# One transpose in place of two for the probabilities of a head, in the attention of a three-layer kernel

## The chip, the cores and the metric

One core of a Trainium2 chip runs the whole kernel. The metric is device microseconds of one execution; the time of a kernel is the median of its executions. The engines are TensorE (PE, with its weight loads shown apart as PEld), VectorE (DVE), ScalarE (ACT), GpSimd (POOL) and SyncE (SP), which issues most transfers.

## The reference

Three layers follow one another: attention with a sink and a sliding window, a mixture of eight experts with one expert a token, and a dense two-layer network.

```python
batch, n_heads, seq, head_dim = (2, 8, 768, 64); n_sink, window = (4, 128)
scores = scale * np.matmul(q, k.transpose(0, 1, 3, 2))
is_sink = pos[None, :] < n_sink
rel = pos[:, None] - pos[None, :]
in_window = (rel >= 0) & (rel < window)
scores = np.where(is_sink | in_window, scores, -1000000000.0)
a = softmax(scores)                        # over the keys
x = np.matmul(a, v)                        # to [1536 tokens, 512]
...
expert_idx = np.argmax(xn @ en.T / tau, axis=1)
out[mask] = gate_w * (np.maximum(x[mask] @ w1[e], 0) @ w2[e])   # for each expert e
...
h = x @ w_in
y = np.maximum(0.01 * h, h) @ w_out
```

## The kernel before

Attention works on units. A unit is one batch b, one group g of four heads and one block i of 128 queries: 2 x 2 x 6 = 24 units, of four heads each, 96 items. With a window of 128, a query block sees two key blocks, its own and the one before; block 0 sees its own alone; blocks 2 to 5 see the sink keys too, which take 32 columns more. `SPAN[i]` says where the keys of block i begin, how many there are, which mask belongs to them, at which columns the key blocks stand (`cols`) and where the sink's columns are.

For an item, `score` makes two TensorE matmuls into `sc` (L276), VectorE adds the mask and takes the extreme into `p` and `los` (L281), and ScalarE takes the exponential in place (L285). `p` holds the four heads of a unit (four buffers). For blocks 2 to 5 GpSimd copies the sink's columns of the four heads together into `sp` (L290), which `flip_sink` turns (L307). `flip` turns each key block of a head with a TensorE transpose into `t` in PSUM (L299), two heads to a tile, and copies the tile to `pt` (L302), by ScalarE for the first pair of heads and by VectorE for the second. `value` multiplies `pt` by the values, eight matmuls of 65 columns and one for the sink (L317, L320). VectorE divides (L329 to L331), and the result is a row block of x, which goes to memory and through the router (`xTp` L729, `lg` L749).

The head's queries and keys are turned beforehand (`tk`, `tq` L206) and split into two parts by ScalarE and VectorE (`head_k` L212 and L217, `head_q` L226 and L229); GpSimd copies `raw_q` (L172) and the sink keys (L220). `stir` issues filler matmuls of 512 columns on a zero tile `warm` in the first steps (L362). `slot_u` (L780) are comparison tables of the router on GpSimd.

The loop over the 96 items is written with lags: at step s, item s is scored, item s - 5 is flipped (`LAG1`), the sink of item s - 7 is turned, and the unit whose last head is item s - 10 is multiplied by the values (`LAG2`). `later(n, fn)` puts a piece of work n steps on. In attention a scheduler then sets the order of each engine's queue from this program; from the experts on TensorE's order is that of the program. The order of units is batch 0 group 0, group 1, then batch 1 in halves; within a group blocks 1 to 5, then 0.

After attention come routing, eight experts (`hp` and `acc`, L1230, L1330, L1348), whose weights SyncE loads into slots as TensorE frees them (L1138, L1181, L1448), and the dense network, which ends the kernel.

`pick` decides, by limits on the inputs, whether a general path runs at the end; with these inputs it does not.

Of the kernel before, what the change touches and what calls it, by code (L numbers as in the profile page):

```python
# [7 lines left out]
F32 = mybir.dt.float32  # L8
F32R = mybir.dt.float32r
BF16 = mybir.dt.bfloat16  # L10
# [5 lines left out]
ALU = mybir.AluOpType  # L16
# [5 lines left out]
P = 128  # L22
# [6 lines left out]
SINK = 32  # L29
# [31 lines left out]
LAG1, LAGS, LAG2, PTB, PB = 5, 7, 10, 6, 4  # L61
HALFK = 3 * P
BEHIND = HALFK + SINK
# [85 lines left out]
def attention(c, ctx):  # L149
# [3 lines left out]
    nc, tc = c.nc, c.tc  # L153
    att = ctx.enter_context(tc.tile_pool(name="a_qk", bufs=4))
    wk = ctx.enter_context(tc.tile_pool(name="a_wk", bufs=2))
    psc = ctx.enter_context(tc.tile_pool(name="ps_sc", bufs=3, space=PSUM))
    c.psc = psc
    pst = c.pst = ctx.enter_context(tc.tile_pool(name="ps_t", bufs=4, space=PSUM))
# [80 lines left out]
    def group_turns(b, g):  # L239
# [4 lines left out]
    load_qk(0, 0, 0, 3)  # L244
    load_qk(0, 1, 0, 3)
    copied = c.copied
    c.warm = c.setting.tile([P, 512], BF16, name="warm")
    nc.vector.memset(c.warm, 0.0)
    setup(c)
    W3 = 2 * P + SINK  # L250


    SPAN = [(0, P, c.m0, [0], None), (0, 2 * P, c.m1, [0, P], None), (P, W3, c.ma, [0, P], 2 * P),
            (2 * P, W3, c.mb, [0, P + SINK], P), (HALFK, W3, c.mc, [SINK, P + SINK], 0),
            (BEHIND + P, W3, c.ma, [0, P], 2 * P)]
    units = {}
    after = []

    def later(n, fn):

        if n == 0:
            return fn()
        after.append((step[0] + n, c.uid(), fn))

    def score(b, g, i, h):
        if h == 0:
            u = units[b, g, i] = Ctx()
            u.p = wk.tile([P, 4, W3], F32, tag="p", name=f"p{b}{g}{i}", bufs=PB)
            u.pt = {}
        u = units[b, g, i]  # L270
        off, n, m, _, s0 = SPAN[i]
        kt, qt = heads[b, 4 * g + h]
        sc = psc.tile([P, W3], F32, tag="sc", name=f"sc{b}{g}{i}{h}")
        w = max(n, 2 * P)
        for half in range(2):
            nc.tensor.matmul(sc[:, 0:w], lhsT=qt[:, half, i * P:(i + 1) * P], rhs=kt[:, off:off + w],  # L276
                             start=half == 0, stop=half == 1)
        p = u.p[:, h, 0:n]
        col = ((b * 2 + g) * QB + i) * 4 + h
        lo = c.los[:, col:col + 1]  # L280
        c.scored = nc.vector.tensor_tensor_reduce(out=p, in0=sc[:, 0:n], in1=m, scale=1.0, scalar=3.0e38,  # L281
                                                  op0=ALU.add, op1=ALU.min, accum_out=lo)

        def raised():
            c.raised = nc.scalar.activation(out=p, in_=p, func=AF.Exp, scale=-1.0, bias=lo)  # L285

        later(1, raised)
        if h == 3 and i >= 2:
            u.sp = wk.tile([P, 4, SINK], F32, tag="sp", name=f"sp{b}{g}{i}")
            later(2, lambda: nc.gpsimd.tensor_copy(u.sp, u.p[:, :, s0:s0 + SINK]))  # L290

    def flip(b, g, i, h):
        u = units[b, g, i]
        cols = SPAN[i][3]
        nb = len(cols)
        if h % 2 == 0:
            u.t = pst.tile([P, 2, nb, P], F32, tag="t", name=f"tp{b}{g}{i}{h}")
        for n, o in enumerate(cols):
            nc.tensor.transpose(u.t[:, h % 2, n, :], u.p[:, h, o:o + P], c.ident)  # L299
        if h % 2 == 1:  # L300
            pt = u.pt[h // 2] = wk.tile([P, 2, nb, P], F32, tag="pt", name=f"pt{b}{g}{i}{h}", bufs=PTB)
            (nc.scalar.copy if h == 1 else nc.vector.tensor_copy)(out=pt, in_=u.t)  # L302

    def flip_sink(b, g, i):
        u = units[b, g, i]
        sk = pst.tile([P, P], F32, tag="t", name=f"sk{b}{g}{i}")
        nc.tensor.transpose(sk, u.sp.rearrange("p h s -> p (h s)"), c.ident)  # L307
        u.ps = wk.tile([P, P], F32, tag="ps", name=f"ps{b}{g}{i}")
        nc.scalar.copy(out=u.ps, in_=sk)
# [47 lines left out]
    def stir(n):  # L357
        if not n:
            return
        t = psx.tile([P, 512], F32, tag="x", name=f"stir{c.uid()}")  # L360
        for _ in range(n):
            nc.tensor.matmul(t, lhsT=c.warm[:, 0:P], rhs=c.warm, start=True, stop=True)  # L362

    items = [(b, g, i, h) for b, g, j0, j1 in UNITS for i in TURN[b][j0:j1] for h in range(4)]
    step = [-1]
# [6 lines left out]
    router_tables(c)  # L372
    setting = router_setup(c)
    stir(7)
    n = len(items)
    for m in (2, 0, 2):
        turn[0, 0][0].pop(0)()
        stir(m)
    s = 0
    while s < n or after:  # L380
# [5 lines left out]
        if s < n:  # L386
            b, g, i, h = items[s]
            if s in STIR:
                stir(STIR[s])
            for (nb, ng), at in FETCH.items():  # L390
                for half in range(2):
                    if s == at[half]:
                        load_qk(nb, 2 * ng, 3 * half, 3)
                        load_qk(nb, 2 * ng + 1, 3 * half, 3)
                if s == at[0]:
                    turn[nb, ng] = group_turns(nb, ng)
                if s == at[2]:
                    load_v(nb, ng)
            for k, at in TURNS.items():
                for half in range(2):  # L400
                    if s in at[half]:
                        turn[k][half].pop(0)()
            score(b, g, i, h)
            if s == 1:
                with tc.issue_after(copied.ins):
                    c.others()
        if 0 <= s - LAG1 < n:
            flip(*items[s - LAG1])
# [11 lines left out]
def pick(c, T, over):  # L420

    nc = c.nc
    part, big, ok = T([P, 1], "part"), T([P, 1], "big"), T([P, 4], "ok")
    nc.vector.tensor_reduce(out=part, in_=c.los, axis=AX.X, op=ALU.max)
    rows = c.ptr.tile([P, P], F32, tag="tr", name="rows_ps")
    nc.tensor.matmul(rows, lhsT=part.to_broadcast([P, P]), rhs=c.ident, start=True, stop=True)
    nc.vector.tensor_reduce(out=big, in_=rows, axis=AX.X, op=ALU.max)
    ns, win = c.ints[:, 0:1], c.ints[:, 1:2]  # L430
    nc.vector.tensor_scalar(out=ok[:, 0:1], in0=ns, scalar1=float(SINK), scalar2=None, op0=ALU.is_le)
    nc.vector.tensor_scalar(out=ok[:, 1:2], in0=win, scalar1=float(P + 1), scalar2=ok[:, 0:1], op0=ALU.is_le, op1=ALU.mult)
    nc.vector.tensor_scalar(out=ok[:, 2:3], in0=win, scalar1=1.0, scalar2=ok[:, 1:2], op0=ALU.is_ge, op1=ALU.mult)
    nc.vector.tensor_scalar(out=ok[:, 3:4], in0=big, scalar1=TOP, scalar2=ok[:, 2:3], op0=ALU.is_lt, op1=ALU.mult)
    nc.vector.tensor_scalar(out=ok[:, 0:1], in0=over, scalar1=0.0, scalar2=ok[:, 3:4], op0=ALU.is_le, op1=ALU.mult)
    nc.vector.tensor_scalar(out=ok[:, 1:2], in0=ok[:, 0:1], scalar1=-1.0, scalar2=1.0, op0=ALU.mult, op1=ALU.add)
    nc.vector.tensor_copy(c.rare, ok[0:1, 1:2])
# [814 lines left out]
class Flow:  # L1252
# [5 lines left out]
    def later(self, n, fn):  # L1258
        self.n += 1
        self.due.append((self.now + n, self.n, fn))  # L1260
# [438 lines left out]
```

## Time and profile before

| | |
|---|---|
| median of 3 runs | 594.13 us (592.95 to 597.09) |
| profiled execution | 593.38 us |
| its span, first to last instruction | 591.6 us |
| PE busy | 579.3 us (98%) |
| DVE, ACT, POOL busy | 375.1, 278.1, 64.7 us |
| TensorE clock granted, mean | 0.998 of full |

Busy times of TensorE contain modelled ends of pipelined matmuls. The chain of waits is followed back from the last instruction, to what released each step or to the instruction before it on the same engine; a piece there has only the time that it adds.

### The profile page before, as it was taken

To read this page: it belongs to the slowest core of one execution; us is meant where nothing else is said; L and a number is where in the kernel's file an instruction comes from. 1 tells how busy PE (TensorE), PEld (TensorE's weight loads), DVE (VectorE), ACT (ScalarE), POOL (GpSimd) and SP (SyncE) were. 2 spreads that over 40 slices of the span, in tenths; PEclk is the share of its full clock that TensorE was granted. 3 is DMA by queue.
4 is the path that set the end of the run, shared out by engine and by line. 5 is a ranking of instruction groups with operands and counts; after the bars stand their busy time and mean duration, and the time that the engine had idled before them with its cause. 6 is when DMAs were issued, how large, how long until landed. Compare 5 with 4: busy or idle time off the path is not lost.

```text
span 591.6 us, 9764 instructions
## 1 busy us (share of the span) xinstructions
PE 579.3 (98%) x3504; PEld 516.1 (87%) x3505; DVE 375.1 (63%) x903; ACT 278.1 (47%) x532; POOL 64.7 (11%) x195
## 2 busy tenths in 40 slices
PE   8999999999999999999999999999999999999995
PEld 5998999999999998899999888888888888888884
DVE  7999699776689966887991799954322223322240
ACT  4878687663476436744552545423322222322220
POOL 6223012121301000010000000000100001100001
PEclk9999999999999999999999999999999999999999
DMA  7646142082295569999977500000100000100001
GB/s 160 154 95 130 61 113 65 24 285 90 77 315 168 157 173 302 350 376 364 377 268 226 202 1 0 2 0 19 54 0 1 0 1 24 48 0 1 0 20 58
DMA packets 75178, 70.44 MB, mean 119 GB/s; under 512 B 41236, under 2 KB 57620, under 8 KB 75120
## 3 DMA queue, kind: packets, MB, share of 16 engines
q1 hardware_dynamic: 72736, 63.07, 34.4%
q0 software_dynamic: 2096, 6.64, 3.4%
q8 instruction: 30, 0.49, 0.3%
q14 instruction: 28, 0.23, 0.1%
q10 hardware_dynamic: 288, 0.00, 0.0%
HBM read 63.41 MB, written 6.29 MB: 118 GB/s over the span
## 4 chain that ended last, share of the span: by engine, by line
PE 86%; DVE 4%; issue 3%; DMA 3%; ACT 2%; SPq 1%; POOL 0%; DVEq 0%; POOLq 0%; ACTq 0%
PE hp L1230 29%; PE acc L1230 28%; PE xp L317 6%; PE hp L1330 4%; PE acc L1348 4%; PE sc L276 4%; PE tp L299 3%; PE lg L749 2%; DMA slot_first<-in_moe_w 1%; PE tq L206 1%; PE xp L320 1%; PE xTp L729 1%; PE tr L1218 1%; PE tk L206 1%; DVE head_k L217 1%
## 5 line engine op out<-in xcount | busy, mean ns | idle before, releaser
L1230 PE MATMUL acc<-slot,h 128*128 128x512 f32 x588 | 142.7, 390 | 0.0
L1230 PE MATMUL hp<-fxT,slot 128*128 128x512 f32 x576 | 137.1, 389 | 0.0
L1230 PEld LDWEIGHTS acc<-slot,h 128*128 128x128 f32 x588 | 109.6, 188 | 22.3
L1230 PEld LDWEIGHTS hp<-fxT,slot 128*128 128x128 f32 x576 | 108.1, 188 | 22.4
L1595 DVE TENSOR_TENSOR lk<-hp,lk 128x512 f32<-128x512 f32 x48 | 32.9, 689 | 97.5 <-ACT lk L1594 97.3
L1594 ACT ACTIVATE lk<-hp 128x512 f32<-128x512 f32 x48 | 28.5, 598 | 110.3 <-PE hp L1230 104.5
L285 ACT ACTIVATE p<-p,los 128x288 f32<-128x288 f32 (+2 forms) x96 | 46.1, 506 | 15.3 <-DVE los L281 14.3
L1150 DVE TENSOR_TENSOR slot<-slot_raw,slot 128x1024 fp32r<-128x1024 f32 x36 | 42.9, 1220 | 4.7 <-ACT slot L1149 4.6
L276 PE MATMUL sc<-head_k,head_q 128*128 128x288 f32 (+1 forms) x192 | 44.9, 332 | 0.6 <-DVE los L281 0.4
L1629 POOL DMA_INDIRECT out_y<-y,sid x12 | 11.7, 978 | 304.2 <-DVE y L1628 282.9
L317 PE MATMUL xp<-v,pt 128*128 128x65 f32 x352 | 44.2, 269 | 0.6 <-DVE x L331 0.5
L317 PEld LDWEIGHTS xp<-v,pt 128*128 128x128 f32 x352 | 42.8, 191 | 1.0 <-PE rk L766 0.6
L1597 DVE TENSOR_TENSOR h<-lk,h 128x512 fp32r<-128x512 f32 x43 | 29.5, 690 | 18.1 <-ACT h L1596 17.9
L1596 ACT CAST h<-lk 128x512 fp32r<-128x512 f32 x43 | 26.7, 622 | 29.2 <-DVE lk L1595 29.2
L1149 ACT CAST slot<-slot_raw 128x1024 fp32r<-128x1024 f32 x36 | 36.0, 1049 | 0.0
L1348 PE MATMUL acc<-h,slot_raw 128*128 128x184 f32 (+2 forms) x192 | 33.8, 320 | 0.1
L276 PEld LDWEIGHTS sc<-head_k,head_q 128*128 128x128 f32 x192 | 29.0, 190 | 3.7 <-DVE los L281 1.3
L1348 PEld LDWEIGHTS acc<-h,slot_raw 128*128 128x128 f32 x192 | 30.7, 190 | 0.4 <-DVE yT L1354 0.4
L1230 PE MATMUL acc<-h,slot 128*128 128x352 f32 (+1 forms) x192 | 30.7, 309 | 0.0
L299 PE MATMUL tp<-ident,p 128*128 128x128 f32 x176 | 29.8, 274 | 0.3 <-ACT pt L302 0.2
L1230 PEld LDWEIGHTS acc<-h,slot 128*128 128x128 f32 x192 | 28.7, 188 | 0.0
L1246 POOL DMA_INDIRECT rows<-xd,ids x15 | 15.5, 1030 | 112.0 <-PE tr L1218 103.3
(294 smaller groups left out, 910.3 us busy)
## 6 DMA issues: line engine op xcount, KB each, us to landing
slot_raw<-in_moe_w SPq DMA_DIRECT2D x48, 512.0 KB
slot_first<-in_moe_w SPq DMA_DIRECT2D x16, 512.0 KB
slot_wide<-in_moe_w_in SPq DMA_DIRECT2D x8, 1024.0 KB
slot_wide<-in_moe_w_out SPq DMA_DIRECT2D x8, 1024.0 KB
raw_k<-in_k SPq DMA_DIRECT2D x32, 96.0 KB
raw_q<-in_q SPq DMA_DIRECT2D x32, 96.0 KB
xd<-x SPq DMA_DIRECT2D x12, 256.0 KB
v<-in_v SPq DMA_DIRECT2D x12, 192.0 KB
```

The lines of the kernel that those rows point to most:

```text
L276: nc.tensor.matmul(sc[:, 0:w], lhsT=qt[:, half, i * P:(i + 1) * P], rhs=kt[:, off:off + w], start=half == 0, stop=half == 1)
L285: c.raised = nc.scalar.activation(out=p, in_=p, func=AF.Exp, scale=-1.0, bias=lo)
L299: nc.tensor.transpose(u.t[:, h % 2, n, :], u.p[:, h, o:o + P], c.ident)
L317: nc.tensor.matmul(xp[:, h, :], lhsT=u.pt[h // 2][:, h % 2, n, :], rhs=vT[b, g][:, kb, h, :], start=h == 0 and n == 0, stop=h == 3 and i < ...
L1149: nc.scalar.copy(out=sl.g[0], in_=raw)
L1150: nc.vector.tensor_tensor(out=sl.g[1], in0=raw, in1=sl.g[0].bitcast(F32), op=ALU.subtract)
L1230: c.nc.tensor.matmul(out, lhsT=a[x], rhs=b[y], start=first and n == 0, stop=last and n == 2)
L1348: nc.tensor.matmul(acc[k], lhsT=g[:, f % 2, k * P:(k + 1) * P], rhs=h, start=f == 0, stop=f == nf - 1)
L1594: nc.scalar.activation(out=raw, in_=hp, func=AF.Copy, scale=0.01)
L1595: nc.vector.tensor_tensor(out=raw, in0=hp, in1=raw, op=ALU.max)
L1596: x = nc.scalar.copy(out=h[:, 0, :], in_=raw)
L1597: y = nc.vector.tensor_tensor(out=h[:, 1, :], in0=raw, in1=h[:, 0, :].bitcast(F32), op=ALU.subtract)
```

## The change

For blocks 2 to 5 (the third to the sixth) the two key blocks of a head are added, for two heads at once, by GpSimd, into 128 columns of `p` (`to` in `SPAN`); the window leaves each query and key offset in at most one of the two. TensorE turns the sum once. Two triangular masks, `sep`, made at the start by VectorE, part it again into the two blocks of `pt`: for the first pair of heads ScalarE copies the tile into the second half of `pt` and GpSimd multiplies it by each mask; for the second pair one VectorE multiplication reads the tile twice and writes both halves. `warm` is 128 columns wide instead of 512 and is read four times over. The general path is now taken for windows over 128, not over 129.

```diff
-    c.warm = c.setting.tile([P, 512], BF16, name="warm")
+    c.warm = c.setting.tile([P, P], BF16, name="warm")
...
-    SPAN = [(0, P, c.m0, [0], None), (0, 2 * P, c.m1, [0, P], None), (P, W3, c.ma, [0, P], 2 * P),
-            (2 * P, W3, c.mb, [0, P + SINK], P), (HALFK, W3, c.mc, [SINK, P + SINK], 0),
-            (BEHIND + P, W3, c.ma, [0, P], 2 * P)]
+    SPAN = [(0, P, c.m0, [0], None, None), (0, 2 * P, c.m1, [0, P], None, None), (P, W3, c.ma, [0, P], 2 * P, P),
+            (2 * P, W3, c.mb, [0, P + SINK], P, 0), (HALFK, W3, c.mc, [SINK, P + SINK], 0, SINK),
+            (BEHIND + P, W3, c.ma, [0, P], 2 * P, P)]
+    sep = c.masks.tile([P, 2, P], BF16, name="sep")
+    nc.vector.tensor_scalar(out=sep[:, 0, :], in0=c.iota, scalar1=c.rowi, scalar2=None, op0=ALU.is_lt)
+    nc.vector.tensor_scalar(out=sep[:, 1, :], in0=c.iota, scalar1=c.rowi, scalar2=None, op0=ALU.is_ge)
...
+        if h % 2 and to is not None:
+            two = u.p[:, h - 1:h + 1]
+            later(2, lambda: nc.gpsimd.tensor_tensor(out=two[:, :, to:to + P], in0=two[:, :, cols[0]:cols[0] + P],
+                                                     in1=two[:, :, cols[1]:cols[1] + P], op=ALU.add))
 
     def flip(b, g, i, h):
         u = units[b, g, i]
-        cols = SPAN[i][3]
+        cols, to = SPAN[i][3], SPAN[i][5]
+        if to is not None:
+            return flip_both(u, b, g, i, h, to)
...
+    def flip_both(u, b, g, i, h, to):
+        if h % 2 == 0:
+            u.t = pst.tile([P, 2, P], F32, tag="t", name=f"tp{b}{g}{i}{h}")
+        nc.tensor.transpose(u.t[:, h % 2, :], u.p[:, h, to:to + P], c.ident)
+        if h % 2 == 0:
+            return
+        pt = u.pt[h // 2] = wk.tile([P, 2, 2, P], F32, tag="pt", name=f"pt{b}{g}{i}{h}", bufs=PTB)
+        if h == 1:
+            nc.scalar.copy(out=pt[:, :, 1, :], in_=u.t)
+            for n in range(2):
+                nc.gpsimd.tensor_tensor(out=pt[:, :, n, :], in0=pt[:, :, 1, :], in1=sep[:, n:n + 1, :].to_broadcast([P, 2, P]), op=ALU.mult)
+        else:
+            nc.vector.tensor_tensor(out=pt.rearrange("p h a q -> p a h q"), in0=u.t.rearrange("p h (o q) -> p o h q", o=1).to_broadcast([P, 2, 2, P]),
+                                    in1=sep.rearrange("p a (o q) -> p a o q", o=1).to_broadcast([P, 2, 2, P]), op=ALU.mult)
...
-            nc.tensor.matmul(t, lhsT=c.warm[:, 0:P], rhs=c.warm, start=True, stop=True)
+            nc.tensor.matmul(t.rearrange("p (a q) -> p a q", a=4), lhsT=c.warm, rhs=c.warm.rearrange("p (o q) -> p o q", o=1).to_broadcast([P, 4, P]),
+                             start=True, stop=True)
...
-    nc.vector.tensor_scalar(out=ok[:, 1:2], in0=win, scalar1=float(P + 1), scalar2=ok[:, 0:1], op0=ALU.is_le, op1=ALU.mult)
+    nc.vector.tensor_scalar(out=ok[:, 1:2], in0=win, scalar1=float(P), scalar2=ok[:, 0:1], op0=ALU.is_le, op1=ALU.mult)
```

## Rows read from the trace of the kernel before

**Rows 1.** The page's part 1, busy time and share of the span by engine:

```profile
PE 579.3 (98%) x3504; PEld 516.1 (87%) x3505; DVE 375.1 (63%) x903; ACT 278.1 (47%) x532; POOL 64.7 (11%) x195
```

**Rows 2.** The chain's shares by line, 53 to 144 us, then 20 to 53:

```profile
by line: PE xp L317 31.3%; PE sc L276 17.1%; PE tp L299 13.9%; PE lg L749 10.6%; PE xp L320 6.2%; PE xTp L729 6.2%; PE tq L206 5.5%; PE tk L206 2.6%; PE sk L307 1.7%; issue 1.6%; DVE pt L302 1.1%; PE fill L841 1.0%; PE tr L1218 0.5%; DVE x 
by line: PE xp L317 25.6%; PE sc L276 15.5%; PE tp L299 12.5%; DVE p L281 7.0%; DVE head_k L217 6.8%; PE tq L206 6.0%; PE xp L320 4.3%; PE tk L206 4.0%; DVE pt L302 3.7%; ACT head_k L212 2.9%; DVE head_q L229 2.8%; issue 2.2%; ACT sq L625 2
```

**Rows 3.** Pieces of the chain: start us, us that each adds:

```profile
49.08 0.47 DVE head_q L229
...
84.24 0.44 PE tp L299 x4
```

**Rows 4.** Busy us of PE, PEld, DVE, ACT, POOL in three stretches, clock, DMA:

```profile
20.00:44.00 24.00, 23.45 (x200) 22.86 (x199) 23.14 (x93) 19.50 (x47) 6.80 (x25) 1.00 0.62 134
44.00:53.00 9.00, 8.97 (x70) 8.00 (x68) 8.06 (x28) 7.66 (x17) 2.65 (x14) 1.00 0.49 111
53.00:115.00 62.00, 61.23 (x522) 59.05 (x520) 51.86 (x212) 46.92 (x114) 12.33 (x40) 1.00 0.32 78
```

**Rows 5.** Groups of PE, 53 to 144 us: busy us, mean ns:

```profile
L299 PE MATMUL tp<-ident,p 128*128 128x128 f32 x112 | 19.5, 274 | 0.0
```

**Rows 6.** Groups of ACT and of DVE, whole span, shapes apart:

```profile
L302 ACT COPY pt<-tp 128x512 f32<-128x512 f32 x20 | 11.6, 579 | 6.9 <-PE tp L299 6.8
...
L302 ACT COPY pt<-tp 128x256 f32<-128x256 f32 x4 | 1.5, 368 | 1.3 <-PE tp L299 1.3
...
L1595 DVE TENSOR_TENSOR lk<-hp,lk 128x512 f32<-128x512 f32 x48 | 32.9, 689 | 97.5 <-ACT lk L1594 97.3
...
L302 DVE COPY pt<-tp 128x512 f32<-128x512 f32 x20 | 13.7, 685 | 1.0 <-PE tp L299 0.9
...
L645 DVE TENSOR_SCALAR tri<-iota,rowi 128x128 bf16<-128x128 f32 x1 | 0.2, 157 | 0.0
```

**Rows 7.** Groups of POOL, whole span, shapes apart:

```profile
L780 POOL TENSOR_SCALAR slot_u<-iota,rp,token 128x128 f16<-128x128 f32 x10 | 7.9, 794 | 25.8 <-DVE rp L776 11.9 <-DVE mine L827 9.3 <-PE tq L206 4.7
...
L290 POOL COPY sp<-p 128x128 f32<-128x128 f32 x16 | 4.7, 294 | 26.4 <-ACT p L285 26.4
...
L124 POOL TENSOR_SCALAR ma<-keep 128x256 f32<-128x256 f32 x1 | 0.4, 407 | 0.1
...
L124 POOL TENSOR_SCALAR ma<-sink 128x32 f32<-128x32 f32 x1 | 0.2, 218 | 0.1
```

**Rows 8.** Groups between 20 and 200 us, the sink transposes' weight loads:

```profile
L307 PEld LDWEIGHTS sk<-ident,sp 128*128 128x128 f32 x16 | 2.4, 152 | 0.5 <-POOL sp L290 0.4
```

**Rows 9.** Instructions of DVE, POOL, ACT and PE in order of time:

```profile
96.53 0.45 DVE L281 CUSTOM_DVE_ANT_0 p<-sc,mb 128x288 f32<-128x288 f32 x1
...
103.28 0.45 DVE L281 CUSTOM_DVE_ANT_0 p<-sc,ma 128x288 f32<-128x288 f32 x1
...
100.72 4.70 POOL L780 TENSOR_SCALAR slot_u<-iota,rp,token 128x128 f16<-128x128 f32 x6 [4.67 <-PE tq L206]
...
120.88 0.46 DVE L281 CUSTOM_DVE_ANT_0 p<-sc,mb 128x288 f32<-128x288 f32 x1
...
121.38 0.54 ACT L285 ACTIVATE p<-p,los 128x288 f32<-128x288 f32 x1 [3.34 <-DVE los L281]
122.21 0.98 ACT L285 ACTIVATE p<-p,los 128x288 f32<-128x288 f32 x2 [0.29 <-DVE los L281]
...
122.86 0.39 PE L299 MATMUL tp<-ident,p 128*128 128x128 f32 x2
...
130.32 0.28 DVE L281 CUSTOM_DVE_ANT_0 p<-sc,m 128x128 f32<-128x128 f32 x1
```

**Rows 10.** Pieces of the chain after attention:

```profile
144.14 1.03 PE hp L1330 x8
...
274.16 8.21 DMA slot_first<-in_moe_w
```

**Rows 11.** What SyncE's queue waited for: us in total, times, longest:

```profile
SPq L1138 <- PE hp L1230: 40.9, 12, 6.1
```

More of the change, by code (lines that the diff above doesn't have):

```diff
@@ L270, in score @@
         u = units[b, g, i]
-        off, n, m, _, s0 = SPAN[i]
+        off, n, m, cols, s0, to = SPAN[i]
         kt, qt = heads[b, 4 * g + h]
```

## The prediction

> **What bounds the kernel now.** Part 1 of the page first: TensorE (PE) is busy 98% of the span [rows 1], but ends of matmuls are modelled, so the chain of waits has to say where it is the bound. Two stretches of the chain differ. From 53 to 144 us, the larger part of attention, the shares by line are TensorE's nearly alone; the transposes of probabilities (`tp`, L299) have 13.9% of 91 us, 12.6 us, and issue and `pt` copies 1.6% and 1.1% [rows 2]. From 20 to 53 us VectorE's lines (`p` L281, `head_k` L217, `head_q` L229, `pt` L302) and ScalarE's `head_k` stand among them, over a fifth of the stretch [rows 2]; a piece such as the 0.47 us of `head_q` at 49.08 is VectorE alone holding the end [rows 3]. The stretches by busy time agree: VectorE (DVE) is busy 23.14 of 24.00 us and 8.06 of 9.00 before 53 us, but 51.86 of 62.00 after [rows 4]. The clock is 1.00 in all of these stretches, the 2.4 GHz level [rows 4]. So there are two regimes: until 53 us two engines are nearly full, and after it one.
>
> **What a transpose costs.** Its record is 274 ns [rows 5], most of it latency. On the chain, where each piece counts only what it adds, four take 0.44 us [rows 3]: 0.11 each. The 112 transposes after 53 us [rows 5] at 0.11 are 12.3 us, and the chain's 12.6 agrees; so there each one counts in full.
>
> **Removed.** Blocks three to six are units with i from 2 to 5: 4 blocks x 4 groups x 4 heads = 64 heads, each with one transpose instead of two. Units with two blocks have 8 transposes and the four with one have 4, 176 in sum; 112 stay, and 64 x 0.11 = 7.0 us leaves TensorE. By the order of units and the 112 counted after 53 us (of which 28 belong to i = 0 and 1 of batch 1 and to i = 0 of the second group), 42 removed ones lie after 53 us and 22 before. After: 42 x 0.11 = **4.6 us**, counted in full. Before: 22 x 0.11 = 2.4 us of TensorE, but VectorE loses no work there, and can catch up only by what it idles: 0.86 + 0.94 = 1.8 us [rows 4]. Bounds 0 and 1.8; I take the middle, **0.9**, since some of that idle time is waiting for TensorE and some for ScalarE.
>
> **Evictions.** For h = 1 ScalarE copies 128x256 instead of 128x512: 368 for 579 ns [rows 6], 16 x 0.21 = 3.4 us less ScalarE. It is behind TensorE after 53 us and worth nothing there; before, it is inside the 0 to 1.8. For h = 3 VectorE multiplies 512 columns from PSUM instead of copying them: 689 ns (a multiply-like form with one PSUM operand) for 685 [rows 6], 16 x 0.004 = 0.1 us, nothing. Both hold for patterns that repeat columns only if repetition is free; the rows show none here, bounds 0 and 0.2 us each, I take 0.
>
> **Setup.** `sep` is two VectorE comparisons of the form of `tri`, 157 ns each [rows 6]; `warm` becomes a quarter as wide. VectorE waits for the first DMAs then, so 0; without that cover 0.3 us. The filler matmuls keep 512 columns; window's limit is a constant.
>
> **Added on GpSimd (POOL).** Per unit two additions of 128x256 (h odd, issued two steps after the score) and two multiplications of 128x256 (h = 1): 16 x 4 = 64 instructions. No two-input POOL instruction is in the trace. One-input ones take 407 ns for 256 columns and 218 for 32: 0.84 ns a column over a fixed 0.19 us [rows 7]. Low bound 0.41 us each, if the second operand is free. High bound: `slot_u` (L780) takes 794 ns where the fit gives 0.30 for 128 columns, 2.65 times; 2.65 x 0.41 = 1.08. I take 0.62, the fixed part and two columns' time for each column (0.19 + 256 x 1.68 ns), because plain arithmetic is nearer to the first row than to a comparison with two pointers. In sum 64 x 0.62 = 40 us, 26 to 69, in some 120 us where POOL works 12.33 of 62 [rows 4]: hidden on average. Where is it dense? The last three units with the change (i = 3, 4, 5 of batch 1, group 1) have their first `p` at 120.88 and the next unit's at 130.32 [rows 9], 3.1 us a unit. POOL needs 4 x 0.62 + 0.29 for `sp` [rows 7] = 2.8 us, just under; at 1.08 it needs 4.6.
>
> The Trainium skill (GPSIMD Engine Reference, Performance versus the Vector engine) speaks against such use: an addition of two float32 tensors costs GpSimd about 2.6 cycles an element at 1.2 GHz, twice VectorE's time, and elementwise work belongs on VectorE. My estimate from it is 0.19 + 256 x 2.17 ns = 0.75 us, so 3.3 us a dense unit, over its 3.1; the sum would then lose 3 x 0.2 = 0.6 us more. No run here shows it yet.
>
> **New waits.** (1) The first head's transpose must now wait for the second head's exponential and the addition. In the dense stretch the first exponential begins at 121.38 and takes 0.54, and its transposes start at 122.86, 0.94 us after it ended [rows 9]. The second ends near 122.75, the addition near 123.4: some 0.6 us late with the hand-over. Behind a transpose in TensorE's queue stand scores, values and router work, all of which wait. Units overlap, so I count this once, where the stretch starts: **-0.6**; bounds 0 and 32 x 0.6 = 19 us (a rival below). (2) POOL takes instructions in order; behind an addition that waits for ScalarE stand `raw_q` copies, `head_k` casts, `sp`, `slot_u`, the gather; TensorE's turns, scores and sink transposes wait for these. Today TensorE's weight loads for `sk` idled 0.4 us for `sp` in all 16 units [rows 8], so such steps run ahead of need. The exception is the burst of six `slot_u`, 4.70 us from 100.72 [rows 9], in the middle of i = 3 and 4 of group 0: two units of POOL work, 5.6, plus 4.7 is 3.5 us more than the 6.8 us in which their scores come (96.53 to 103.28 [rows 9]). Bounds 0 and 3.5. Four buffers of `p` allow transposes to come a unit late, so nearer to 0: **-0.7**. (3) The multiplications stand between ScalarE's copy and the values, which come five steps after the last transposes: covered by that lag; without it 1.2 us a unit.
>
> **Does the gain last?** After 144 us the order of TensorE is fixed by hand. The expert weights are asked for after the routing, and one of the loads is on the chain, at 274.16 for 8.21 us [rows 10]. That would swallow a gain if the transfers had their own pace, but SyncE waits 40.9 us for TensorE to free slots in one of its lines alone [rows 11]: transfers start when TensorE lets them, and move with it. The early expert's loads are first used at 144.14 [rows 10]; the routing that releases them moves by the gain made before it, all but 12 x 0.11 = 1.3 us, so they are no later relative to need by more than that. I count the gain as kept.
>
> **The sum.** 4.6 + 0.9 - 0.6 - 0.7 = 4.2 us. The profiled execution took 593.38 us (591.6 span and 1.8 around it), so 589.2; the median of the runs is 594.13, 0.75 above, so **589.9** for a median.
>
> **Rivals.** A: every removed transpose pays, 7.0 us: 587.1. For it: `tp` has 12.5% of the chain from 20 to 53 us too [rows 2]. Against: VectorE's 1.8 us of idleness. B: the gain is eaten where another engine is close, VectorE in 53 to 115 us (84%) and the burst in full (3.5 us): 4.6 - 0.6 - 3.5 = 0.5, or 593.6. C, slower: TensorE's queue is drawn up ahead, and if its place for a transpose allows for a shorter addition than the real one, it stands in front of each of the 32 pairs with w us. Gross gain 5.5; it breaks even at w = 0.17, and is 1% slower from w = 0.36. With the addition at 1.08 instead of 0.62, w = 0.46: 32 x 0.46 - 5.5 = +9.2, 603.3. For it: the gap of 0.94 us; against: the sink path, where such a place allowed enough. That fewer transposes are not run at all is excluded by the code.
>
> **How the numbers follow.** Forecast 0.48 (587.5 to 591.5), A 0.17, B 0.18 (592 to 597), C 0.17 (598 to 606). 1% is 5.9 us, about what measuring tells from no change (the runs spread over 4.1 us). Below 588.2: most of A and a sixth of the forecast, 0.23. Above 600.1: most of C, 0.14. The rest 0.63. The range reaches from 1.1 us beyond A, 586.0, a third of the way into C, 601.0: outside are 0.04 below and 0.12 above.
>
> **What would show it.** Right: 112 `tp` transposes, still 0.11 each on the chain; POOL additions of 0.41 to 1.08 us; first expert work (`hp` L1330) some 4 us before 144.14; chain from 20 to 53 us richer in VectorE. Wrong: TensorE idle for POOL at L299's successor (C); POOL over 90% busy from 120 to 135 us; or a first expert that starts earlier while the end does not move, the weights being late.

## The result, and the profile after

Nine runs of the changed kernel have a median of 603.63 us (598.93 to 605.85), beside 594.13 (592.95 to 597.24) for nine of the kernel before in the same job; the ratio is 1.014 [1.011, 1.017]. The forecast was 589.9 in a range of 586.0 to 601.0: the change costs 9.5 us where 4.2 were to be gained. The profiled execution took 602.3 us, its span 600.4.

Part 1 of the page after, to be held against [rows 1]: TensorE is still busy 97%, GpSimd (POOL) 106.6 us instead of 64.7. The second line is TensorE's granted clock from part 2, in 40 slices of 15 us. The slice from 120 us is at 6.

```profile
PE 583.2 (97%) x3441; PEld 513.7 (86%) x3441; DVE 375.8 (63%) x905; ACT 273.7 (46%) x532; POOL 106.6 (18%) x259
...
PEclk9999999969999999999999999999999999999998
```

The chain's shares by line, 53 to 152 us and then 20 to 53, answer [rows 2]. In the first stretch the transposes (`tp`, now L316 and L308) have 8.0% where 13.9% stood; new in both is a DMA of `raw_q`, and in the first VectorE's `p`.

```profile
by line: PE xp L341 28.4%; PE sc L279 10.9%; PE lg L774 8.4%; PE xp L344 6.3%; PE xTp L754 5.5%; DVE p L284 4.8%; PE tp L316 4.3%; DMA raw_q<-in_q 3.8%; issue 3.7%; PE tp L308 3.7%; PE tq L206 3.6%; DVE x L355 2.4%; DVE head_k L217 2.2%; PE
by line: PE sc L279 28.0%; PE xp L341 26.2%; DMA raw_q<-in_q 11.3%; PE tq L206 9.0%; PE tp L316 6.0%; PE xp L344 5.8%; PE tk L206 5.5%; PE tp L308 4.3%; ACT head_q L226 2.7%; ACT p L288 1.5%; issue 1.5%; DVE p L284 1.4%; PE sk L331 1.0%; PE
```

The groups of the new work, shapes apart, answer [rows 5] to [rows 7] (busy us, mean ns, idle before and releaser). The count of removed transposes and the small prices are as forecast; VectorE's multiplication, 682 ns, costs no more than its copy did.

```profile
L296 POOL TENSOR_TENSOR p<-p 128x256 f32<-128x256 f32 x32 | 23.5, 736 | 7.6 <-ACT p L288 7.5
L323 POOL TENSOR_TENSOR pt<-pt,sep 128x256 f32<-128x256 f32 x32 | 21.5, 674 | 10.9 <-ACT pt L321 10.3
...
L316 PE MATMUL tp<-ident,p 128*128 128x128 f32 x64 | 13.3, 276 | 2.3 <-POOL p L296 2.2
L325 DVE TENSOR_TENSOR pt<-tp,sep 128x512 f32<-128x512 f32 x16 | 10.9, 682 | 2.5 <-PE tp L316 2.4
...
L321 ACT COPY pt<-tp 128x256 f32<-128x256 f32 x16 | 5.9, 367 | 4.4 <-PE sk L331 1.6 <-PE tp L316 1.4 <-POOL pt L323 1.3
```

Busy time by stretch (us of PE, PEld, DVE, ACT, POOL, then the clock, DMA share and GB/s); the first three lines answer [rows 4]. Ahead of them stand two stretches of the kernel before, to hold the later ones against:

```profile
98.00:118.00 20.00, 19.47 (x164) 18.57 (x163) 15.98 (x73) 13.70 (x35) 5.47 (x9) 1.00 0.07 27
118.00:130.00 12.00, 11.62 (x99) 10.97 (x99) 8.73 (x47) 6.80 (x17) 3.36 (x5) 1.00 0.79 256
```

The changed kernel:

```profile
20.00:44.00 24.00, 22.44 (x170) 19.97 (x168) 23.44 (x96) 20.32 (x52) 16.05 (x41) 1.00 0.64 137
44.00:53.00 9.00, 9.00 (x77) 8.53 (x77) 7.73 (x26) 4.98 (x11) 4.19 (x14) 1.00 0.32 73
53.00:115.00 62.00, 57.60 (x471) 53.69 (x469) 49.24 (x200) 43.51 (x108) 32.96 (x74) 1.00 0.31 82
98.00:102.00 4.00, 3.38 (x23) 2.64 (x21) 3.97 (x15) 2.36 (x7) 2.15 (x4) 1.00 0.01 2
102.00:106.00 4.00, 3.03 (x21) 2.38 (x20) 2.07 (x11) 2.05 (x5) 4.00 (x6) 1.00 0.17 66
106.00:110.00 4.00, 3.28 (x28) 3.07 (x29) 1.21 (x3) 1.63 (x5) 3.71 (x7) 1.00 0.17 66
110.00:114.00 4.00, 3.89 (x32) 3.48 (x31) 2.92 (x12) 2.04 (x6) 1.34 (x2) 1.00 0.00 0
114.00:118.00 4.00, 2.60 (x18) 1.92 (x19) 3.02 (x13) 3.25 (x11) 1.71 (x4) 1.00 0.00 0
118.00:122.00 4.00, 4.00 (x22) 3.62 (x22) 1.62 (x9) 0.24 (x2) 0.61 (x1) 0.61 0.01 4
122.00:126.00 4.00, 3.67 (x20) 3.52 (x19) 2.46 (x21) 0.80 (x2) 1.58 (x2) 0.50 0.02 3
126.00:130.00 4.00, 3.85 (x22) 3.05 (x21) 1.79 (x7) 0.54 (x1) 0.00 (x0) 0.61 0.96 323
```

TensorE idled 0.77 us in 53 to 115; now it idles 4.4. Then, from 118 to 130, its records fill the time again, but at a granted clock of 0.50 to 0.61, the 1.2 GHz level for most of it: with a mean of 0.57, 0.43 of 12 us is missing there, 5.1 us of work at full clock. A busy share alone hides this; only the clock's column and the lengths of equal pieces show it. On the chain the 16 matmuls of a unit's values take 1.73 us at 60.68, but 2.66 and 3.65 here:

```profile
60.68 1.73 PE xp L341 x16
...
117.75 2.66 PE xp L341 x16
...
122.85 3.65 PE xp L341 x16
...
152.45 1.03 PE hp L1355 x8
```

The last line answers [rows 10]: the first expert starts at 152.45, not 144.14, and the span's end is 8.8 us later: what attention loses, the end loses. SyncE's wait for slots is 40.6 us, as in [rows 11]. GpSimd in order of time, 100 to 109 us (start, us), answers the burst of [rows 9]:

```profile
100.38 0.67 POOL L323 TENSOR_TENSOR pt<-pt,sep 128x256 f32<-128x256 f32 x1 [1.71 <-ACT pt L321]
101.19 4.68 POOL L805 TENSOR_SCALAR slot_u<-iota,rp,token 128x128 f16<-128x128 f32 x6
105.84 0.66 POOL L323 TENSOR_TENSOR pt<-pt,sep 128x256 f32<-128x256 f32 x1
106.45 0.28 POOL L293 COPY sp<-p 128x128 f32<-128x128 f32 x1
106.70 1.40 POOL L296 TENSOR_TENSOR p<-p 128x256 f32<-128x256 f32 x2
108.06 0.28 POOL L293 COPY sp<-p 128x128 f32<-128x128 f32 x1
108.31 1.40 POOL L296 TENSOR_TENSOR p<-p 128x256 f32<-128x256 f32 x2
```

The second multiplication of a unit (105.84) stands behind six tables that it does not need, and four additions behind it. TensorE's timeline shows a weight load that waits for that multiplication, and a transpose that waits for an addition:

```profile
106.67 0.97 PEld L341 LDWEIGHTS xp<-v,pt 128*128 128x128 f32 x8 [1.39 <-POOL pt L323]
```
```profile
115.10 0.41 PE L316 MATMUL tp<-ident,p 128*128 128x128 f32 x2 [1.20 <-POOL p L296]
```

The second wait is not one behind the tables. That addition stands behind a sink copy for which GpSimd itself had idled 1.74 us until ScalarE's `p` came:

```profile
114.04 0.29 POOL L293 COPY sp<-p 128x128 f32<-128x128 f32 x1 [1.74 <-ACT p L288]
```

Nor is all of the idle time in 98 to 118 GpSimd's. From 95.46 to 103.22 the chain runs nearly all through VectorE's lines, two of them here, and VectorE is busy 3.97 of 4 us from 98 on:

```profile
97.28 0.55 DVE head_k L217
...
98.44 0.69 DVE pt L325
```

A second place is earlier. On the chain at 51 to 57 us stand a DMA, the copy on GpSimd that waits for it, a sink copy, and an addition that needs neither the DMA nor the copies:

```profile
51.24 3.73 DMA raw_q<-in_q
...
55.02 0.13 POOL raw_q L172
...
55.30 0.29 POOL sp L293
55.60 0.70 POOL p L296
...
56.34 0.33 PE tp L316
```

### The profile page after: what moved, and what is told of

It reads as the page before. It is cut to its first block, busy times and chain, and to the rows that moved or that the text cites. A ratio compares the mean times of both kernels' runs of the same rounds, so it can differ in the third digit from the quotient of the medians.

```text
span 600.4 us, 9699 instructions
## 1 busy us (share of the span) xinstructions
PE 583.2 (97%) x3441; PEld 513.7 (86%) x3441; DVE 375.8 (63%) x905; ACT 273.7 (46%) x532; POOL 106.6 (18%) x259
## 4 chain that ended last, share of the span: by engine, by line
PE 89%; DVE 4%; DMA 3%; issue 2%; ACT 1%; POOL 0%; SPq 0%; DVEq 0%; POOLq 0%; ACTq 0%
PE hp L1255 28%; PE acc L1255 28%; PE xp L341 6%; PE hp L1355 6%; PE acc L1373 5%; PE sc L279 4%; PE tq L206 2%; PE lg L774 1%; PE xp L344 1%; PE tr L1243 1%; PE stir L386 1%; PE tp L316 1%; PE tp L308 1%; PE xTp L754 1%; PE tk L206 1%
## 5 line engine op out<-in xcount | busy, mean ns | idle before, releaser
L341 PE MATMUL xp<-v,pt 128*128 128x65 f32 x352 | 46.2, 281 | 1.7 <-DVE x L355 1.6
L341 PEld LDWEIGHTS xp<-v,pt 128*128 128x128 f32 x352 | 44.4, 201 | 2.9 <-POOL pt L323 1.4
L296 POOL TENSOR_TENSOR p<-p 128x256 f32<-128x256 f32 x32 | 23.5, 736 | 7.6 <-ACT p L288 7.5
```

The source lines that it names most:

```text
L341: nc.tensor.matmul(xp[:, h, :], lhsT=u.pt[h // 2][:, h % 2, n, :], rhs=vT[b, g][:, kb, h, :], start=h == 0 and n == 0, stop=h == 3 and i < ...
```

## The experiments

Three theories stood after the result. **Queue**: additions and multiplications are held up on GpSimd's in-order queue by other work, TensorE idles, and the clock falls after it. **VectorE**: with fewer transposes VectorE is the bound near 100 us (3.97 of 4 us at 98), whatever GpSimd does. **Pair**: each addition and multiplication costs its own short wait. The expectations of e1 to e4 call the first the burst theory; those from e5 on add a **clock** theory, in which fewer transposes alone leave TensorE idle and the clock falls for that. Hunks are cut short. The kernel before ran in each job, with medians of 593.9 to 596.1, so the ratios are against its runs in the same job.

Two measures are used beside the medians. Runs of one kernel differ with their mean granted clock: the changed kernel took 598.93 us at 0.993 and 605.85 at 0.979. Within the kernels here, over all their runs, a mean clock lower by 0.001 went with 0.52 us; "at 0.998" or "at one clock" below is a kernel's mean time moved along that line (the kernel before: 593.7; the changed one: 596.2), an estimate. And "score 45" and "score 81" are the starts of those scores on VectorE after the first one, in the profiled run: 55.4 and 109.3 us before, 55.9 and 117.8 after. So the two batches can be read apart: 0.5 us is lost up to score 45, 8.0 from there to score 81.

**Without additions and multiplications; without one kind (e1 to e3).**

```diff
-            later(2, lambda: nc.gpsimd.tensor_tensor(... op=ALU.add))
-            for n in range(2):
-                nc.gpsimd.tensor_tensor(out=pt[:, :, n, :], ... op=ALU.mult)
...
-        nc.tensor.transpose(u.t[:, h % 2, :], u.p[:, h, to:to + P], c.ident)
+        nc.tensor.transpose(u.t[:, h % 2, :], u.p[:, h, SPAN[i][3][1]:SPAN[i][3][1] + P], c.ident)
...
-                nc.tensor.matmul(xp[:, h, :], lhsT=u.pt[h // 2][:, h % 2, n, :], rhs=vT[b, g][:, kb, h, :],
+            for n, kb in enumerate(pair):
+                nc.tensor.matmul(xp[:, h, :], lhsT=u.pt[h // 2][:, h % 2, 1 if h < 2 and i > 1 else n, :], rhs=vT[b, g][:, kb, h, :],
```

These are hunks of e1. In e2 the transpose reads `SPAN[i][3][0]` and the multiplications stay; in e3 the additions and the transpose stay. All three leave work out, so they give prices and not the result.

> Left out: GpSimd's 32 additions and its 32 multiplications, with the 64 removed transposes still gone. One block's probabilities are turned unsummed, the first pair of heads reads one copy for both blocks, and the value blocks read are chosen so that the experts' loads keep fitting; every other instruction is as in the changed kernel. The burst theory (six slot_u tables hold the additions and multiplications on GpSimd's in-order queue, TensorE waits, then its granted clock falls to 1.2 GHz): nothing stands behind the burst any more but the sink copies, so the first expert starts 3 to 7 us before 144.1, no stretch of 118 to 130 has a clock under 0.9, and the time is 587 to 591. The VectorE theory (VectorE, at 3.97 of 4 us in 98:102, is the bound and TensorE starves behind it whatever GpSimd does): TensorE has less work and VectorE the same, so the idle time and the fall of the clock stay, and the time is 596 to 604. The pair theory (every addition and multiplication costs TensorE a short wait, all along): 587 to 591 as well, and the next two runs share the loss in proportion to their counts.

> Left out: GpSimd's 32 additions alone; one block's probabilities are turned unsummed, and the value blocks read are chosen so that the experts' loads keep fitting. The 32 multiplications stay. The burst theory: the multiplications still stand behind the six tables, a unit's first pair is late by up to 4.7 us as at 100.38 to 105.84, and the time is 594 to 600. The VectorE theory: 600 to 604. The pair theory: with the wait of the transposes on the additions gone (3.0 us in 3 waits before 150 us) 592 to 597.

> Left out: GpSimd's 32 multiplications alone; the first pair of heads of a unit reads the summed, unparted copy for both blocks, and the value blocks read are chosen so that the experts' loads keep fitting. The additions stay. The burst theory: the additions of two units still stand behind the six tables, so the transposes wait as at 106.7 to 108.3, and the time is 594 to 602. The VectorE theory: 600 to 604. The pair theory: 592 to 598, since half of GpSimd's 45 us is gone.

Measured: 590.74 us (0.9922 [0.9899, 0.9946] of before), 589.27 (0.9918 [0.9896, 0.9941]) and 593.87 (0.9969 [0.994, 0.9999]); at 0.998: 587.7, 588.8 and 590.6. The VectorE theory falls as the whole cause: without GpSimd's work the same VectorE work fits (first expert at 138.4). The change without GpSimd's work is worth 6.0 us at one clock. Either kind alone takes back 1.1 (multiplications) or 2.9 (additions); the pair theory wanted the shares to add up, but together they take back 8.4 (596.2). So the price is in their company on one queue. The queue theory missed too: it had 594 to 600 and 594 to 602 for the single kinds, and multiplications alone behind the tables came out 4.7 us below its range; additions alone are inside the pair theory's 592 to 598. And the clock fell in the first run too, at 134 to 146 us, with nothing of the new work on GpSimd:

```profile
134.00:140.00 6.00, 6.00 (x31) 5.36 (x31) 2.61 (x19) 1.71 (x6) 1.58 (x2) 0.58 0.12 47
140.00:146.00 6.00, 5.70 (x48) 4.98 (x47) 4.00 (x24) 1.11 (x4) 0.00 (x0) 0.85 0.02 4
```

**The tables on VectorE (e4); the tables spread (e8).**

```diff
-            (nc.vector if late else nc.gpsimd).tensor_scalar(out=c.u[:, t], ...)
+            nc.vector.tensor_scalar(out=c.u[:, t], ...)
```

> The changed kernel, complete, with all twelve slot_u tables on VectorE, where two of them took 0.33 us each; six of them then cost VectorE 2.0 us near 100 us and GpSimd nothing. The burst theory: no operation stands in front of the additions and multiplications, the items 74 to 80 are late by 1 to 2 us in place of 4.5 to 8.0, the clock stays at 1.0 and the time is 589 to 595. The VectorE theory: 2.0 us more on the engine that ends last there, 603 to 606. The pair theory: 600 to 604.

```diff
+            def both(u=u):
+                x = nc.gpsimd.tensor_tensor(out=two[...], ..., op=ALU.add)
+                if c.tables:
+                    with tc.issue_after(x.ins):
+                        c.tables.pop(0)()
+            later(2, both)
...
+        if t <= RANKS[0]:
+            c.tables.append(table)
+            continue
```

> The changed kernel with the six first slot_u tables issued one at a time, each behind one of GpSimd's additions, in place of six in a row (4.68 us at 101.19). The same work on the same engine. The queue theory: no addition or multiplication stands behind more than one table of 0.79 us, so the hold-up of some 4 us near 101 to 108 shrinks to about 1 and the time is 596 to 600; less comes back than if the multiplications were gone, since they still stand in front of the additions. The clock theory: the idle time of TensorE in 98:118 that is VectorE's remains, the clock falls, 601 to 605.

On VectorE: 599.01 us (1.0066 [1.0038, 1.0093]), neither what the queue theory expected (589 to 595) nor the others. The 2.0 us fall where VectorE has no room; it is busy 8.00 of 8 us from 98 to 106 and TensorE 2.63 of the first 4, and the clock is 0.65 in 106 to 118. At 0.998 the run is at 594.9, so most of its miss is the clock's. It doesn't separate the theories. Spread: 596.43 (1.0033 [1.0004, 1.0062]), as the queue theory expected. GpSimd does the same work, but the multiplication that had waited until 105.84 now runs at 102.79 and the first two additions at 103.65 and 105.14, not from 106.70 on:

```profile
101.23 1.59 POOL L813 TENSOR_SCALAR slot_u<-iota,rp,token 128x128 f16<-128x128 f32 x2
102.79 0.66 POOL L330 TENSOR_TENSOR pt<-pt,sep 128x256 f32<-128x256 f32 x1
103.40 0.28 POOL L294 COPY sp<-p 128x128 f32<-128x128 f32 x1
103.65 0.72 POOL L298 TENSOR_TENSOR p<-p 128x256 f32<-128x256 f32 x1
104.36 0.80 POOL L813 TENSOR_SCALAR slot_u<-iota,rp,token 128x128 f16<-128x128 f32 x1
105.14 0.71 POOL L298 TENSOR_TENSOR p<-p 128x256 f32<-128x256 f32 x1
...
```

TensorE still idles in 98 to 106, where VectorE ended most of its waits (busy 6.73 of 8 us; the changed kernel had 6.41). From 106 to 118 it is busy 11.46 of 12 us, where the changed kernel had 9.77. The clock then stays up where it had fallen:

```profile
118.00:122.00 4.00, 3.62 (x33) 3.33 (x34) 3.03 (x23) 0.62 (x2) 1.58 (x2) 1.00 0.12 36
122.00:126.00 4.00, 3.82 (x26) 3.09 (x25) 3.51 (x18) 2.85 (x7) 2.96 (x5) 1.00 1.00 337
126.00:130.00 4.00, 4.00 (x34) 3.82 (x34) 2.70 (x15) 3.87 (x11) 4.00 (x7) 1.00 1.04 368
```

From score 45 to score 81 it takes 54.2 us, the kernel before 53.9, the changed one 61.9. So the order of the tables makes nearly all of the second batch's loss: 7.2 us between the medians, of which 2.5 remain at one clock and the rest is the clock. The clock theory (601 to 605 here) falls as the whole cause.

**Unused matmuls in the gap (e7); both cures (e12).**

```diff
+            if 66 <= s < 86:
+                fill(c, pst, "t", 1)
             score(b, g, i, h)
```

> The changed kernel with one more matmul of 512 columns (0.22 us, result unused) ahead of the score of each of the items 66 to 85, from about 94 to 130 us: 20 of them, 4.4 us of TensorE's time, most of it where TensorE stood idle (5 to 6 us in 98:118). The clock theory: the clock stays at 1.0 in 118:130, the 5.6 us lost there come back less 1 to 2 us of the matmuls that fall where TensorE was full, 598 to 600. The queue theory: the additions come as late as before, the matmuls fill waits only, and of the fall a part comes back at best, 600 to 606.

> The changed kernel, complete, with both the spread tables and the 20 unused matmuls of 512 columns. Each alone gave 596.4 and 596.6 against 603.6. If waits and clock are two separate losses (4 us of waits near the tables, 6 to 7 us of fallen clock), the two mend different parts and the time is 592.5 to 594.5. If both mend the same loss, 595 to 597.

Measured: 596.60 us (1.0046 [1.0021, 1.0071]) and 594.76 (0.9999 [0.9974, 1.0024]). The first is better than any theory had it: 4.4 us of useless work made the kernel 7.0 us faster. Its clock is 1.00 in 118:130, and six of its ten runs had 0.998 or 0.999, at 595.33 to 596.64: about the changed kernel with the clock's share taken out, for which the line above gives 596.2.

```profile
118.00:130.00 12.00, 11.43 (x87) 9.70 (x85) 9.84 (x57) 5.73 (x15) 6.04 (x9) 1.00 0.56 186
```

The second lies 0.3 us above what separate losses would give and 0.2 below what one loss would. It doesn't decide. A part in common would fit, since the spread tables remove a cause of the gap that the matmuls fill.

**Part of the units (e9 to e11).**

```diff
+    def way(b, g, i):
+        return b == 0
...
+        to = to if way(b, g, i) else None
```

The last line stands in `score` and in `flip`. The late units are `b == 1`; the six are (0,1,5), (1,0,2) and (1,1,2) to (1,1,5).

> Complete computation. The new way only for the eight units of the first batch (scores up to 67 us), the eight of the second as before: 32 transposes fewer, 16 additions and 16 multiplications, none of them near the slot_u tables. Two-place theory (the changed kernel loses about 5.6 us against the run without additions and multiplications at 45 to 61 us, where the additions stand in one queue with copies that wait for DMAs, and about 9 us at 98 to 130, in waits and in the clock): the item 44 is scored at 66.5 to 67.5 us as before, nothing of the 3.5 us of 32 transposes is left, 593 to 595. One-place theory (all of the loss is made behind the tables at 101 us): the 32 transposes pay in part, 590 to 592.5.

> Complete computation. The new way only for the eight units of the second batch (scores from 72 us on), the eight of the first as before. Two-place theory: up to 72 us as before; then 32 transposes fewer (3.5 us) against waits of 4 to 5 us and a clock that falls near 106 to 126, 598 to 604. One-place theory: the same or somewhat worse than the changed kernel, 602 to 606. Were the loss an even price per addition and multiplication, half of it: 598 to 599.

> Complete computation. The new way only for six of sixteen units, those whose turning falls where TensorE was full and GpSimd little used in the kernel before (60 to 94 us: 20.00 of 20 us and 2.54 of 20 us; 122 to 134: 12.0 of 12 and 2.1 of 12): 24 transposes fewer, 2.6 us of TensorE. Queue theory: no addition stands behind a copy that waits or a table, TensorE does not idle, so most of it pays, 591 to 592.5. If fewer transposes are worth nothing whatever GpSimd does, or bring a fall of the clock by themselves: 594 to 598.

Measured: 594.07 us (0.9979 [0.9956, 1.0003]), 602.63 (1.0139 [1.0096, 1.0183]) and 593.73 (0.9974 [0.9952, 0.9995]). The first batch gets next to nothing for 32 transposes (score 45 at 56.2, 0.7 us at one clock), as the two-place theory expected; the second makes the whole loss, with a clock of 0.60 in 118:130 of its profile, a time that both place theories allowed. An even price for each addition (598 to 599) is out. Where GpSimd had been nearly idle and TensorE full, 1.7 us of the 2.6 are gained at one clock, but the median is above the 591 to 592.5 that the queue theory expected.

**The first pair's parting taken off GpSimd.** By VectorE (e6), or by turning that pair as before: in all units (e5), in the first batch alone (e16), in the first batch with the whole new way where it paid in the second (e13).

```diff
-        if h == 1:
-            nc.scalar.copy(out=pt[:, :, 1, :], in_=u.t)
...
-        else:
+        if True:
             nc.vector.tensor_tensor(out=pt.rearrange("p h a q -> p a h q"), ...)
```

> Complete computation. The first pair is parted by VectorE straight from the transposes' tile, as the second is: GpSimd has the 32 additions and no multiplication, ScalarE loses 16 copies of 0.37 us, VectorE gains 16 operations of 0.69 us (11 us, some 2 us of them in 94 to 106, where it is full). The queue theory: GpSimd's queue is that of the run without multiplications (593.9), plus up to 4 us of VectorE, 592 to 598. The clock theory: TensorE's idle time near 100 us is VectorE's making, so it grows, 602 to 606. If VectorE's total decides, at 0.98 busy in 20:44 and 3.97 of 4 us in 98:102, 604 or more.

```diff
-        if h % 2 and to is not None:
+        if h == 3 and to is not None:
...
-        if to is not None:
+        if to is not None and h > 1:
             return flip_both(u, b, g, i, h, to)
```

> Complete computation. Only the second pair of heads of a unit goes the new way (16 additions on GpSimd, parted by VectorE's multiplication); the first pair is turned as before, four transposes and a ScalarE copy, so 32 transposes are removed, there are no multiplications on GpSimd and half of the additions. The queue theory (the loss is made by additions that stand behind multiplications and tables on GpSimd's in-order queue; either kind alone costs little): half of the gain of the run without either kind, so 590 to 593. The clock theory (fewer transposes leave TensorE idle near 100 us, the granted clock falls, and that fall is the loss): TensorE has 3.5 us less work than before, one fall of 3.5 to 4 us, 594 to 598. The pair theory (every addition costs a wait): half of the loss of the changed kernel, 597 to 600.

> Complete computation. As e9, but only for the second pair of heads: 16 transposes fewer (1.8 us), 8 additions on GpSimd, no multiplication on it. The copies of raw_q stay. If the number of GpSimd's operations in the early stage decides, all of the 1.8 us and what the order gives back is gained: item 44 some 2 us earlier than before (55.4 us after the first item), 591.5 to 592.5. If an addition behind a waiting copy is enough to lose it: 593.5 to 594.5.

> Complete computation. In the first batch the new way for the second pair of heads only (no multiplication on GpSimd), in its unit of scores 40 to 43 and in five of eight units of the second batch the whole new way, in the three units turned near the slot_u tables the old way: 42 transposes fewer, 4.6 us. From the runs with the parts alone, each read at one granted clock: the first batch gained 2.3 us in the run with the second pairs, six units 1.7 us, of which one unit is in both: 3.5 us, 590 to 591.5. If the gains don't add up, because the fewer transposes bring a fall of the clock (3 to 4 us each) that the kernel before has in a quarter of its runs: 592 to 595.

On VectorE it is 1.0173 [1.0118, 1.0229] of before (603.21 to 607.28 us in three of its four runs, 617.07 in the fourth): score 45 already comes at 60.6 us, 5.2 late. The queue theory's 592 to 598 was wrong, since VectorE had 1.8 us to spare in 20 to 53 us [rows 4]. But part of the 5.2 us is the clock again, which was 0.86 in 20 to 44, some 3 us of that stretch; at 0.998 the run is at 597.0.

```profile
20.00:44.00 24.00, 21.44 (x145) 19.83 (x144) 22.76 (x85) 15.51 (x40) 10.13 (x29) 0.86 0.62 134
```

Second pairs in all units: 596.78 (1.0034 [1.0004, 1.0064]) where the queue theory had 590 to 593 and the clock theory 594 to 598. At 0.998 it would be 591.8, so the miss is the clock's, whose means lie between 0.978 and 0.995. What its profile, one of the runs at 0.995, shows of a gap is that the burst holds its additions too, and TensorE is busy 3.15 and 2.98 us in 98:102 and 102:106; that this gap makes the fall in the other runs is not shown.

```profile
98.29 4.71 POOL L805 TENSOR_SCALAR slot_u<-iota,rp,token 128x128 f16<-128x128 f32 x6
102.97 0.72 POOL L296 TENSOR_TENSOR p<-p 128x256 f32<-128x256 f32 x1
```

Second pairs in the first batch alone: 591.38 (0.9946 [0.9923, 0.9968]; 591.5 to 592.5 was expected if the number of operations decides), score 45 at 53.1, 2.3 us earlier than before, and TensorE busy 16.76 us of 44:61 instead of 16.20. The mixture: 592.43 (0.9948 [0.9921, 0.9974]), 590.0 at 0.998: the parts do add up at one clock, but eight of its twelve runs had 0.992 or 0.993, so the median is in the range that was given for a fall of the clock (592 to 595), not in 590 to 591.5. Both beat the kernel before by half a per cent, and by their medians the changed one by 2%.

**The copies that wait for a DMA,** in e9's kernel (e14) and, as a control, in the kernel before (e15):

```diff
-            c.copied = nc.gpsimd.tensor_copy(rq[:, c0:c0 + n, j, 1, :], rq[:, c0:c0 + n, j, 0, :])
+            if (b, pr) in ((0, 0), (0, 1)):
+                c.copied = nc.gpsimd.tensor_copy(rq[:, c0:c0 + n, j, 1, :], rq[:, c0:c0 + n, j, 0, :])
+            else:
+                nc.sync.dma_start(out=rq[:, c0:c0 + n, j, 1, :],
...
```

> The kernel of e9 (the new way in the first batch alone, 594.07) without GpSimd's 24 copies of raw_q for the later groups of heads: a second DMA brings the same rows in their place. Complete computation. If additions and multiplications are held up behind copies that wait for their DMA (as at 55.02), the item 44 is scored 2 to 4 us earlier than in e9 (56.1 us after the first item) and the time is 590 to 592; set against the control e15. If it is the number of operations, of which 16 additions and 16 multiplications (22.6 us) outweigh the 24 copies (8.4 us), under 1 us comes back: 593 to 594.

> Control: the kernel before without the same 24 copies of raw_q, a second DMA in their place. GpSimd was used a sixth of that stage, nothing waited behind the copies but sink copies and memsets; so the time is that of before within 1 us either way, 593 to 595, where the DMAs (0.6 busy in 20:60) don't delay what follows them.

Measured: 593.59 us (0.9973 [0.9948, 0.9997]) and 594.73 (1.0001 [0.9975, 1.0026]). Score 45 moves from 56.2 to 54.9, and in the control stays at 55.4; at 0.998 the times are 592.3 and 593.4, against 593.0 for e9. So copies are 0.7 to 1.3 us of the early loss of some 5 (score 45 is at 50.8 without GpSimd's new work, at 55.9 with it), not the 2 to 4 expected if the waiting copies were the cause; the time is the one given for the number of operations (593 to 594). With them gone, GpSimd's line from 49.95 to 58 is still one addition, cast and multiplication after another. What remains was removed only by having fewer of them (53.5 with multiplications alone, 54.4 with additions alone, 53.1 with 8 additions and 16 transposes fewer). Which of these operations holds which, the runs don't settle.

## Why the prediction was wrong

**The step that failed** is the one on new waits, (1) to (3), with -0.6, -0.7 and nothing, and the sentence "hidden on average" ahead of it. At one clock the 64 GpSimd instructions cost 8.4 us (596.2 against 587.7), not 1.3. The larger part, some 5 us, is lost before score 45 (50.8 us in e1, 55.9 in the changed kernel), where (2) put the price at nothing because the sink copies of the kernel before ran ahead of need; which operation holds which there stays open. The error was not in their price: 736 and 674 ns, 45.0 us in sum against 40 forecast and 26 to 69 as bounds. Spare time of an in-order queue is no cover by itself; near 101 us what counted was what stood in front. The prediction named the burst and bounded it by 3.5 us, took 0.7 because four buffers of `p` would allow it, and in (3) held the multiplications covered by the values' lag: the one at 105.84 was caught behind the burst, and the values waited for it at 106.67. At one clock the burst cost 2.5 us (e8), inside that bound.

**What the prediction didn't have at all** is the clock. It read 1.00 in every stretch before and carried that over. TensorE, busy 16.18 of 20 us in 98:118, then worked at the 1.2 GHz level in most of 118:130. That the gap brought the fall is shown by e7, which fills it, and by e8, which removes its later part. The medians of the runs' clocks are 0.985 and 0.997; twelve steps of 0.52 us are 6.2 us, more than the loss of the burst itself. Not all of it can be put down to GpSimd: without its work (e1) the median is still 0.991, and e8's profiled run, which keeps 1.00 in 118:130, falls to 0.73 and 0.70 in 140:146 and 146:152. What brings those falls is open. So the sum, put right: -6.0 for the transposes, +8.4 for GpSimd, +6.2 for the clock: +8.6, beside 9.5 measured.

**Early gain, 0.9 us, and 4.6 us counted in full.** As the worth of the transposes alone their sum was right: 5.5 forecast, 6.0 at one clock (e1). The split was not, so the sum is in part luck: in e1 score 45 comes 4.6 us earlier than before, more than the 3.5 us of the first batch's 32 transposes, and only 0.9 more is gained up to score 81 (103.8 us, 109.3 before). VectorE, nearly full before 53 us, did not hold the early gain down as the prediction had it. In the changed kernel the early part was lost to GpSimd (e9). The chain from 20 to 53 us did not get richer in VectorE, as the prediction said to look for; VectorE's `p` fell from 7.0 to 1.4% and a DMA has 11.3%.

**Kept after 144 us**: right. The first expert came 8.3 us later, and the span's end 8.8.

**The price of one operation.** An addition took 736 ns where 0.62 was taken. The Trainium skill's figure (GPSIMD Engine Reference, Performance versus the Vector engine), from which the estimate of 0.75 us was worked out, agrees with the trace for the addition; a multiplication took 674 ns. Its advice to do such work on VectorE brought nothing here: with the partings on VectorE (e6) the kernel took 1.0173 [1.0118, 1.0229] of before, where the changed kernel took 1.014 [1.011, 1.017].

**Rivals.** C had the right side and nearly the right time (603.3), by another mechanism: TensorE waited for additions three times before 150 us, 3.0 us in all, not at each of 32 pairs. B named the burst, but with its 3.5 us alone would have ended at 593.6. The dense stretch came later than the prediction looked for it and did little harm: GpSimd was busy 10.03 of 14 us from 130 to 144, and TensorE 13.70.

## What to carry to other kernels

Before giving an engine more work, list its queue in order around each new instruction: a long run of unrelated instructions, or one that waits for a DMA, delays what comes after it by up to its whole length, whatever the engine's idle share. Spreading that run is cheap and brought back 7.2 us of the 9.5. And where the bounding engine is TensorE, a gap can have a second price, the clock in the stretch that follows; read the granted clock by stretch and by run before a difference of a few us is put down to instructions.

## Not expected of the hardware

Useless matmuls paid: 20 of them made the kernel 7.0 us faster, by holding the granted clock at 1.00 where it had been 0.50 to 0.61. The kernel before has two levels of its own: of its 124 runs beside the experiments 73 had a mean clock of 0.996 or more, with a median of 593.6 us, and 51 less, with 596.9; two medians of a few runs each can differ by 3 us for that alone. And two GpSimd operations on equal shapes differ: 736 ns for the addition of two float32 tiles, 674 for a multiplication by a bfloat16 tile.
